# Weight conversion as single VectorE operations dealt over the mixing steps, VectorE in emission order, three softmax buffers

## The chip, the core and the metric

The kernel runs on one core of one Trainium2 chip. The metric is the device time of one launch in microseconds; lower is better. The core has a matmul engine (TensorE, PE in the rows, its weight loads PEld), VectorE (DVE), ScalarE (ACT), GpSimd (POOL) and SyncE (SP), which here only starts transfers. Each engine takes its own instructions in their order and waits on semaphores for the others.

## What is computed

Two blocks follow each other: an attention that mixes its heads before and after the softmax, and a Fourier mixing with a two-layer network behind it. Batch 8, 12 heads, 448 positions, 64 per head; so 768 channels, and 3072 in the hidden layer.

```python
scores = scale * np.matmul(q, k.transpose(0, 1, 3, 2))
scores = np.einsum('bhij,hg->bgij', scores, w_pre)
scores = scores - np.max(scores, axis=-1, keepdims=True)
attn = np.exp(scores)
attn = attn / (np.sum(attn, axis=-1, keepdims=True) + 1e-09)
attn = np.einsum('bhij,hg->bgij', attn, w_post)
x = np.matmul(attn, v)              # then (B, H, S, D) to (B, S, H*D)
...
X = np.fft.fft(x, axis=1)
X = np.fft.fft(X, axis=2)
u = x + np.real(X)
un = (u - mean(u)) / np.sqrt(var(u) + 1e-06)
out = u + np.maximum(un @ w_ch1, 0.0) @ w_ch2
```

The two weights of the network arrive as 64-bit numbers. The kernel makes 32-bit ones of them on the chip, by operations on the two halves of their bits, and keeps the result in device memory.

## The kernel before

The function `mix_phase` holds the attention, the Fourier mixing and the conversion of the weights; `ffn_phase` holds the network and comes behind it.

**Steps.** The mixing is cut into 192 steps (`TOT`), 24 for each of 8 batches. Step T has a tile of gathered score rows `Kr` (fetched from `Sb` by four transfers that SyncE starts, `emit_gather`), multiplied with `w_pre` on TensorE into the PSUM tile `mx` (*premix*, line 294). VectorE takes the row maximum of `mx` into `nmx` (line 301). ScalarE writes the exponentials into the softmax tile `PP`, with their sums in `den` (line 310). GpSimd adds the small constant to `den` (line 318), VectorE takes the reciprocal `rcp` (line 320), GpSimd scales `PP` with it (line 323). TensorE multiplies `PP` with `w_post` into `po` (*postmix*, line 333), and VectorE writes `po` transposed in blocks into `Pv` (line 344). `mx` and `po` have one buffer each, `PP` two, the PSUM tiles `ms` for everything else four.

**Order of emission.** The loop at the end of `mix_phase` emits step by step. In step s stand, in this order: premix, maximum and exponential of step s + 2 (`LM`), the score matmuls that are due (`emit_qk`, one in every step, two copies from `ms` to `Sb` behind each) or the value product (`emit_av`, every sixth step, copies to `XT`), the postmix and transpose of step s, the scaling of s + 2, the gather of s + 4, and then what is due of the rest: transposes of q and k (`emit_xpose`), the back-transposed output `X` (`emit_x`), the first Fourier transform (`emit_z`, line 416), and the second one with the sum to `X` (`emit_s2`: matmuls at line 436, four additions on VectorE at lines 444 and 447). Each batch has four of these sums, in four steps in a row early in the next batch; the text calls them sum steps. A step with none of the rest and no value product is called bare.

**Who sets the order.** `manual_schedule` keeps TensorE's instructions in the order of emission. On all other engines a scheduler sets the order ahead of time, by its own estimate of when operands are there.

**Copies.** `_Evac` chooses ScalarE or VectorE for the copies out of PSUM by a running sum for each engine. The conversion adds 440 to VectorE's sum for each of its operations.

**Conversion.** `_pieces` cuts the weights into 96 pieces of 128 rows by 384 (48 of `w_ch1`, then 48 of `w_ch2`). `emit_convert` has GpSimd start the load of a piece into `raw64` (line 457), then emits seven VectorE operations (lines 468 to 481) on the tiles `tmp` and `top`, and SyncE's transfer of `top` to `w1f` or `w2f` (line 483). The pool `pcv` has two buffers of each tile. Piece x is due at step 1.9 x (`WSTEP`); its seven operations are emitted together at the end of that step. On VectorE the scheduler moves them to where it expects operands.

## Time and profile before

| | us |
|---|---|
| three runs | 2999.58, 3004.24, 3007.17 |
| median | 3004.24 |
| profiled execution, its own time | 3000.97 |
| its span, first to last instruction | 2999.2 |
| TensorE busy in it | 2610.3 |
| VectorE busy | 1228.7 |
| ScalarE busy | 734.3 |
| GpSimd busy | 649.5 |
| mean granted TensorE clock, of full speed | 0.952 |

The profile is one execution. The page names lines of the kernel; a group of rows below says which view it is. In the timeline a row is a start, a duration, an engine, a line, an operation with its output and inputs, and in brackets the idle time of the engine ahead of it with what ended it. Rows of neighbouring equal instructions are merged (x4 is four). In the windows each engine has its busy time in the stretch, then come the clock that TensorE was granted (1.00 is full speed), the busy share of the DMA engines, and GB/s.

### The profile page before, as it was taken

Reading aid. Unit: us, or ns where it says so; the run is one execution under the profiler, and the core shown is the slowest. Engines: PE = TensorE matmul, PEld = TensorE weight load, DVE = VectorE, ACT = ScalarE, POOL = GpSimd, SP = SyncE. Lnnn points to the kernel's source line nnn. Section 1 sums busy time; section 2 is a strip of 40 time slices with the busy share of each in tenths; the row PEclk is TensorE's granted clock in tenths of the full one; section 3 lists DMA queues with packets and bytes.
Section 4 is the critical chain, followed back from the end, with each engine's and each line's share of the span. In section 5 each row is a group of like instructions: output and inputs, shape, how many; then the busy total and the mean of one; then the engine's idle time right before and its main releaser. Section 6 shows DMA issues by size and latency. Waiting matters only on the chain.

```text
span 2999.2 us, 47325 instructions
## 1 busy us (share of the span) xinstructions
PE 2610.3 (87%) x18992; PEld 1655.9 (55%) x18992; DVE 1228.7 (41%) x2242; ACT 734.3 (24%) x1931; POOL 649.5 (22%) x1101
## 2 busy tenths in 40 slices
PE   4565665979797988878999999999999999999998
PEld 1232322435344444435866866866876876876875
DVE  4878888644444444457430320320320320320220
ACT  2242232454545555531100100100100100100100
POOL 4353344353535434332001001001001001001000
PEclk8687887999999999988999999999999999999999
DMA  7566566443434333348544444444444444444432
GB/s 191 171 174 188 169 189 176 128 130 110 128 100 128 113 108 107 102 158 315 204 164 167 157 153 164 167 153 163 161 160 161 155 162 156 155 164 153 156 107 107
DMA packets 185112, 463.02 MB, mean 154 GB/s; under 512 B 22990, under 2 KB 128974, under 8 KB 172350
## 3 DMA queue, kind: packets, MB, share of 16 engines
q1 hardware_dynamic: 161886, 367.18, 35.4%
q0 software_dynamic: 23008, 92.82, 11.3%
q8 instruction: 151, 2.47, 0.3%
q14 instruction: 67, 0.55, 0.1%
HBM read 317.56 MB, written 59.77 MB: 126 GB/s over the span
## 4 chain that ended last, share of the span: by engine, by line
PE 41%; issue 11%; DMA 7%; ACT 2%; DVE 1%; SPq 1%; POOL 1%; ACTq 0%; POOLq 0%; DVEq 0%
PE psP L715 9%; PE psP L755 8%; PE psR L755 6%; PE psR L715 5%; PE psQ L755 3%; DMA w1t<-w1f 3%; PE psQ L715 2%; DMA out_dram<-u 2%; PE mx L294 1%; PE ms L436 1%; DMA w2t<-w2f 1%; DMA u<-u_scr 1%; ACT PP L310 1%; PE ms L268 1%; PE ms L361 1%
## 5 line engine op out<-in xcount | busy, mean ns | idle before, releaser
L715 PE MATMUL psP<-ub,w1t 128*128 128x256 f32 x2016 | 468.7, 386 | 26.8 <-DVE mv L674 15.1
L715 PEld LDWEIGHTS psP<-ub,w1t 128*128 128x128 f32 x2016 | 385.3, 193 | 95.3 <-DMA w1t<-w1f 24.4
L755 PE MATMUL psP<-w2t,h 128*128 128x384 f32 x1344 | 436.9, 486 | 0.0
L294 PE MATMUL mx<-Kr,kw 60*64 60x448 f32 x1536 | 209.0, 611 | 211.4 <-ACT PP L310 206.6
L755 PEld LDWEIGHTS psP<-w2t,h 128*128 128x128 f32 x1344 | 254.4, 190 | 173.4
L310 ACT ACTIVATE PP<-mx,nmx 128x448 f32<-128x448 f32 x384 | 240.2, 630 | 225.2 <-DVE nmx L301 194.1
L333 PE MATMUL po<-PP,kw 60*32 60x448 f32 x3072 | 209.8, 605 | 95.4 <-DVE Pv L344 71.9
L323 POOL TENSOR_SCALAR PP<-PP,rcp 128x448 f32<-128x448 f32 x384 | 252.8, 667 | 128.5 <-DVE rcp L320 123.8
L692 POOL TENSOR_TENSOR ub<-ub 128x768 f32<-128x768 f32 x28 | 50.8, 1837 | 1058.7 <-ACT ub L687 1058.2
L344 DVE STREAM_TRANSPOSE Pv<-po 128x896 f32<-128x896 f32 x192 | 213.6, 1112 | 157.1 <-PE po L333 157.1
L118 ACT COPY Sb<-ms 124x448 f32<-124x448 f32 x375 | 182.8, 541 | 308.3 <-PE ms L268 282.8
L301 DVE TENSOR_REDUCE nmx<-mx 128x2 f32<-128x896 f32 x192 | 208.6, 1086 | 113.1 <-PE mx L294 113.1
L715 PE MATMUL psR<-ub,w1t 128*128 128x256 f32 x1008 | 232.6, 380 | 0.4 <-DMA w1t<-w1s 0.3
L294 PEld LDWEIGHTS mx<-Kr,kw 60*64 60x64 f32 x1536 | 43.1, 140 | 321.9 <-ACT PP L310 298.8
L755 PE MATMUL psR<-w2t,h 128*128 128x384 f32 x672 | 220.0, 486 | 0.0
L268 PE MATMUL ms<-kT,qT 64*64 64x448 f32 (+1 forms) x1536 | 203.3, 589 | 4.6 <-DVE X L447 3.3
L715 PEld LDWEIGHTS psR<-ub,w1t 128*128 128x128 f32 x1008 | 190.9, 190 | 28.3 <-DMA w1t<-w1s 2.5
L755 PEld LDWEIGHTS psR<-w2t,h 128*128 128x128 f32 x672 | 126.3, 190 | 84.3
L764 DVE TENSOR_TENSOR u<-u,psP 128x384 f32<-128x384 f32 x56 | 31.0, 554 | 341.6 <-PE psP L755 341.6
L333 PEld LDWEIGHTS po<-PP,kw 60*32 60x32 f32 x3072 | 36.8, 109 | 237.0 <-issue 169.3
L361 PEld LDWEIGHTS ms<-Pv,vv 64*64 64x64 f32 x5376 | 154.4, 139 | 21.6 <-issue 17.7
L361 PE MATMUL ms<-Pv,vv 64*64 64x120 f32 x5376 | 157.5, 273 | 3.6 <-DVE Pv L344 1.9
(88 smaller groups left out, 2648.8 us busy)
## 6 DMA issues: line engine op xcount, KB each, us to landing
Kr<-Sb SPq DMA_DIRECT2D x768, 105.0 KB
w2t<-w2s SPq DMA_DIRECT2D x56, 1152.0 KB
w2t<-w2f SPq DMA_DIRECT2D x42, 1152.0 KB
w1t<-w1s SPq DMA_DIRECT2D x72, 576.0 KB
raw<-in_moe_w_ch_dram POOLq DMA_DIRECT2D x96, 384.0 KB, 4.0
w1t<-w1f SPq DMA_DIRECT2D x84, 384.0 KB
w1t<-w1f SPq DMA_DIRECT2D x96, 192.0 KB
w1t<-w1s SPq DMA_DIRECT2D x72, 192.0 KB
```

The lines of the kernel that those rows point to most:

```text
L118: self.nc.scalar.copy(out=out, in_=in_)
L268: nc.tensor.matmul(pss[x][64 * y:64 * y + r0 + 64 - lo, :S], st["qT", xx][64 * x:64 * x + 64, y, lo:r0 + 64], st["kT", xx][64 * x:64 * x + ...
L294: nc.tensor.matmul(mx[64 * z:64 * z + 64, x, :S], kw1[64 * x:64 * x + KR, :], Kr[64 * x:64 * x + KR, z, :], start=True, stop=True)
L301: nc.vector.tensor_reduce(nmx[:, :], steps[T]["mx"][:, :, :S], axis=AX.X, op=ALU.max, negate=True)
L310: nc.scalar.activation(PP[:, x, :], steps[T]["mx"][:, x, :S], ACTF.Exp, bias=steps[T]["nmx"][:, x:x + 1], accum_out=den[:, x:x + 1])
L323: nc.gpsimd.tensor_scalar(PP[:, x, :], PP[:, x, :], rcp[:, x:x + 1], 1.0, op0=ALU.mult, op1=ALU.mult)
L333: nc.tensor.matmul(po[o:o + 32, z, :S], kw2[64 * z:64 * z + KR, y, :], PP[64 * z:64 * z + KR, :, c * HS:(c + 1) * HS], start=True, stop=True)
L344: nc.vector.transpose(g["Pv"][:, T % GT, :].rearrange("p (z s) -> p z s", z=2), steps[T]["po"][:, :, :S])
L361: nc.tensor.matmul(pss[y][64 * x:64 * x + 64, pr * nu * R:(pr + 1) * nu * R], st["v"][64 * y:64 * y + 64, i, jb * D:(jb + 1) * D], _ap(Pv, ...
L692: nc.gpsimd.tensor_tensor(ub[:, o], ub[:, a], ub[:, b], op=ALU.subtract)
L715: nc.tensor.matmul(p, w[m][:, i, kc, :], ub[:, i, kc, :], start=opens and kc == 0, stop=kc == NK - 1, skip_group_check=True)
L755: nc.tensor.matmul(p, lhs[i][:, half * NQ + kf, x * P:(x + 1) * P], w[:, kf, :], start=opens and half == 0 and kf == 0, stop=half == 1 and ...
```

## The change

Three things are changed in `mix_phase`, and the function around it stays.

1. `emit_convert` gives back its seven operations one by one, and `convert(n)` emits the next n of the row of all pieces: the load of a piece is emitted ahead of its first operation, its store behind its last. From step -4 on, each step emits four, one of them between postmix and transpose, three behind the transpose and ahead of the scaling; in a sum step it emits one.
2. `manual_schedule` now names VectorE too, so its instructions stand as they are emitted. The copies and additions behind the rest (`take("full", ...)`) are put off in `pend`: they are emitted ahead of the next piece of the rest, or in the next step behind maximum and exponential.
3. The pool `ppp` of the softmax tile `PP` has three buffers in place of two.

```diff
@@ -52,7 +52,6 @@
 
 
 WC = 384
-WSTEP = 1.9
 
 TB = 512
 NTB = B * S // TB
@@ -147,7 +146,7 @@
     psb = pool("psb", 2)
     pkr = pool("pkr", 3)
     pvv = pool("pvv")
-    ppp = pool("ppp", 2)
+    ppp = pool("ppp", 3)
     psm = pool("psm", 4)
     ppv = pool("ppv", 2)
     pxt = pool("pxt")
@@ -161,6 +160,7 @@
     pms = pool("pms", 4, space=bass.MemoryType.PSUM)
 
     ev = _Evac(nc)
+    pend = []
 
     def ms_tile():
         return pms.tile([P, 512], F32, name="ms", tag="ms")
@@ -381,7 +381,8 @@
                     nc.scalar.copy(out=dst, in_=src)
                 else:
                     nc.vector.tensor_copy(out=dst, in_=src)
-        return [lambda y=y: done(y) for y in range(2)]
+        pend.extend(lambda y=y: done(y) for y in range(2))
+        return []
 
     def emit_x(g):
         X = pxx.tile([GR, DM], F32, name="X", tag="X")
@@ -462,27 +463,45 @@
         tmp = pcv.tile([P, WC], F32, name="tmp", tag="tmp")
         topb, tmpb = top[:, :].bitcast(U32), tmp[:, :].bitcast(U32)
 
-        def done():
-
-
-            nc.vector.tensor_scalar(tmpb, hi, 0x7fffffff, None, op0=ALU.bitwise_and)
-            nc.vector.tensor_scalar(tmp[:, :], tmp[:, :], _f32(0x38000000),
-                                    _f32(0x47efffff), op0=ALU.max, op1=ALU.min)
-
-            nc.vector.tensor_scalar(topb, tmpb, 0x07ffffff, 3, op0=ALU.bitwise_and,
-                                    op1=ALU.logical_shift_left)
-            nc.vector.scalar_tensor_tensor(topb, hi, 0xc0000000, topb,
-                                           op0=ALU.bitwise_and, op1=ALU.bitwise_or)
-
-            nc.vector.tensor_scalar(tmpb, topb, 0xff800000, None,
-                                    op0=ALU.bitwise_and)
-            nc.vector.scalar_tensor_tensor(tmp[:, :], lo, 2.0 ** -52, tmp[:, :],
-                                           op0=ALU.mult, op1=ALU.mult)
-            nc.vector.tensor_tensor(top[:, :], top[:, :], tmp[:, :], op=ALU.add)
+
+
+
+
+        vec = nc.vector
+        ops = [
+            lambda: vec.tensor_scalar(tmpb, hi, 0x7fffffff, None, op0=ALU.bitwise_and),
+            lambda: vec.tensor_scalar(tmp[:, :], tmp[:, :], _f32(0x38000000),
+                                      _f32(0x47efffff), op0=ALU.max, op1=ALU.min),
+            lambda: vec.tensor_scalar(topb, tmpb, 0x07ffffff, 3, op0=ALU.bitwise_and,
+                                      op1=ALU.logical_shift_left),
+            lambda: vec.scalar_tensor_tensor(topb, hi, 0xc0000000, topb,
+                                             op0=ALU.bitwise_and, op1=ALU.bitwise_or),
+            lambda: vec.tensor_scalar(tmpb, topb, 0xff800000, None,
+                                      op0=ALU.bitwise_and),
+            lambda: vec.scalar_tensor_tensor(tmp[:, :], lo, 2.0 ** -52, tmp[:, :],
+                                             op0=ALU.mult, op1=ALU.mult),
+            lambda: vec.tensor_tensor(top[:, :], top[:, :], tmp[:, :], op=ALU.add),
+        ]
+
+        def store():
             ev.d += 7 * 440.0
             nc.sync.dma_start(
                 out=dst, in_=top.rearrange("p (m f) -> p m f", m=split))
-        return [done]
+        return ops, store
+
+    cuts, conv = list(weights), []
+
+    def convert(n):
+
+        for _ in range(n):
+            if not conv and cuts:
+                ops, store = emit_convert(*cuts.pop(0))
+                conv.extend(ops)
+                conv.append(store)
+            if conv:
+                conv.pop(0)()
+            if len(conv) == 1:
+                conv.pop(0)()
 
 
     fill = {"tile": [], "full": [], "none": []}
@@ -512,42 +531,54 @@
             due("full", f + GS + 4 + x // 2,
                 lambda b=b, par=par, ch=ch: emit_z(b, par, ch))
     due("none", 2, emit_tables)
-    for x, cut in enumerate(weights):
-        due("none", x * WSTEP, lambda cut=cut: emit_convert(*cut))
     for v_ in fill.values():
         v_.sort(key=lambda e: (e[0], e[1]))
 
+    def flush():
+        while pend:
+            pend.pop(0)()
+
     def take(kind, s):
-        evs = []
+        n = 0
         while fill[kind] and fill[kind][0][0] <= s:
+            if kind == "full":
+                flush()
             evs = fill[kind].pop(0)[2]()
-            if kind == "none":
-                held.extend(evs)
+            n += 1
+            if kind == "full":
+                pend.extend(evs)
                 continue
             for fn in evs:
                 fn()
-
+        return n
+
+    sums = {f * GS + GS + 8 + n for f in range(B) for n in range(NG)}
     s = int(min(v_[0][0] for v_ in fill.values()))
-    with tc.manual_schedule(engines={mybir.EngineType.PE}):
+    with tc.manual_schedule(engines={mybir.EngineType.PE, mybir.EngineType.DVE}):
         while s < TOT or any(fill.values()):
-            held = []
             take("none", s)
             if 0 <= s + LM < TOT:
                 emit_premix(s + LM)
                 emit_max(s + LM)
                 emit_exp(s + LM)
+            flush()
             take("tile", s)
+            ops = 0 if s < -4 else 1 if s in sums else 4
             if 0 <= s < TOT:
                 emit_postmix(s)
+                convert(min(ops, 1))
                 emit_turn(s)
+                ops -= 1
+            convert(ops)
             if 0 <= s + LM < TOT:
                 emit_scale(s + LM)
             if 0 <= s + LG < TOT:
                 emit_gather(s + LG)
             take("full", s)
-            for fn in held:
-                fn()
             s += 1
+        flush()
+        while conv or cuts:
+            convert(1)
```

What the order of instructions is now, at three places. On VectorE around step 16 of the kernel before, two pieces of weights are converted side by side, as the scheduler set them (`nmx` is the maximum, `rcp` the reciprocal, `Pv` the transpose, all others are conversion):

```order
L344 STREAM_TRANSPOSE Pv_1105<-po_1247 128x896
L469 TENSOR_SCALAR tmp_3655<-tmp_3655 128x384
L320 RECIPROCAL rcp_1258<-den_1145 128x2
L472 TENSOR_SCALAR top_3654<-tmp_3655 128x384
L474 SCALAR_TENSOR_TENSOR top_3654<-raw64_3652,top_3654 128x384
L468 TENSOR_SCALAR tmp_3837<-raw64_3834 128x384
L477 TENSOR_SCALAR tmp_3655<-top_3654 128x384
L469 TENSOR_SCALAR tmp_3837<-tmp_3837 128x384
L301 TENSOR_REDUCE nmx_1276<-mx_1271 128x2
L479 SCALAR_TENSOR_TENSOR tmp_3655<-raw64_3652,tmp_3655 128x384
L472 TENSOR_SCALAR top_3836<-tmp_3837 128x384
L481 TENSOR_TENSOR top_3654<-top_3654,tmp_3655 128x384
```

In the later batches of the kernel before, nothing of this stands between the transposes, reciprocals and maxima. After the change, two steps of the sixth batch on VectorE:

```order
L320 RECIPROCAL rcp_8863<-den_8832 128x2
L301 TENSOR_REDUCE nmx_8877<-mx_8872 128x2
L477 SCALAR_TENSOR_TENSOR top_8857<-raw64_8855,top_8857 128x384
L344 STREAM_TRANSPOSE Pv_8562<-po_8892 128x896
L479 TENSOR_SCALAR tmp_8858<-top_8857 128x384
L481 SCALAR_TENSOR_TENSOR tmp_8858<-raw64_8855,tmp_8858 128x384
L483 TENSOR_TENSOR top_8857<-top_8857,tmp_8858 128x384
L320 RECIPROCAL rcp_8908<-den_8880 128x2
L301 TENSOR_REDUCE nmx_8922<-mx_8917 128x2
L472 TENSOR_SCALAR tmp_8948<-raw64_8945 128x384
L344 STREAM_TRANSPOSE Pv_8950<-po_8936 128x896
```

One piece at a time, four operations a step, the first between maximum and transpose, in every batch.

On ScalarE, around a value product in the middle of the mixing (`PP` is the exponential, `XT` the copies behind the value product, `Sb` the score copies). Before:

```order
L310 ACTIVATE PP_8916,den_8917<-mx_8909,nmx_8914 128x448 x2
L381 COPY XT_9054<-ms_8968 128x3x60
L381 COPY XT_9054<-ms_8969 128x3x60
L118 COPY Sb_8876<-ms_9059 124x448
L118 COPY Sb_8876<-ms_9060 124x448
L310 ACTIVATE PP_8964,den_8965<-mx_8957,nmx_8962 128x448 x2
```

After, the same place:

```order
L310 ACTIVATE PP_8924,den_8925<-mx_8917,nmx_8922 128x448 x2
L310 ACTIVATE PP_8972,den_8973<-mx_8965,nmx_8970 128x448 x2
L381 COPY XT_9062<-ms_8976 128x3x60
L381 COPY XT_9062<-ms_8977 128x3x60
L117 COPY Sb_8883<-ms_9063 124x448
L117 COPY Sb_8883<-ms_9064 124x448
```

The second exponential has moved ahead of the copies of the value product and of the scores.

On VectorE in a sum step late in the mixing (`X` are the four additions). Before:

```order
L320 RECIPROCAL rcp_13140<-den_13118 128x2
L444 TENSOR_TENSOR X_11817<-X_11817,ms_13154 112x385
L447 TENSOR_TENSOR X_11817<-X_11817,ms_13154 112x383
L444 TENSOR_TENSOR X_11817<-X_11817,ms_13149 112x385
L447 TENSOR_TENSOR X_11817<-X_11817,ms_13149 112x383
L301 TENSOR_REDUCE nmx_13176<-mx_13171 128x2
L344 STREAM_TRANSPOSE Pv_12858<-po_13190 128x896
```

After:

```order
L320 RECIPROCAL rcp_13134<-den_13104 128x2
L301 TENSOR_REDUCE nmx_13157<-mx_13152 128x2
L445 TENSOR_TENSOR X_11811<-X_11811,ms_13148 112x385
L445 TENSOR_TENSOR X_11811<-X_11811,ms_13143 112x385
L448 TENSOR_TENSOR X_11811<-X_11811,ms_13148 112x383
L448 TENSOR_TENSOR X_11811<-X_11811,ms_13143 112x383
L483 TENSOR_TENSOR top_13003<-top_13003,tmp_13004 128x384
L344 STREAM_TRANSPOSE Pv_12854<-po_13176 128x896
```

The maximum has moved ahead of the four additions, and one conversion operation stands behind them. That is so behind two of the four sum steps of a batch; behind the two others the additions stay ahead of the maximum.

## Rows read from the trace of the kernel before

**Rows 1.** The page, its first line.

```profile
span 2999.2 us, 47325 instructions
```

**Rows 2.** Timeline of VectorE: the transposes 0, 72, 168 and 191 of 192.

```profile
54.45 1.10 DVE L344 STREAM_TRANSPOSE Pv<-po 128x896 f32<-128x896 f32 x1
...
660.64 1.12 DVE L344 STREAM_TRANSPOSE Pv<-po 128x896 f32<-128x896 f32 x1 [0.54 <-PE po L333]
...
1216.32 1.12 DVE L344 STREAM_TRANSPOSE Pv<-po 128x896 f32<-128x896 f32 x1 [0.54 <-PE po L333]
...
1351.40 1.10 DVE L344 STREAM_TRANSPOSE Pv<-po 128x896 f32<-128x896 f32 x1
```

**Rows 3.** Windows: stretch, length; busy of PE, PEld, DVE, ACT, POOL; clock, DMA, GB/s.

```profile
200.00:300.00 100.00, 56.99 (x715) 24.04 (x723) 77.67 (x157) 30.17 (x83) 43.64 (x72) 0.76 0.63 178
900.00:1000.00 100.00, 84.79 (x1194) 44.07 (x1187) 44.21 (x61) 53.02 (x145) 44.20 (x83) 1.00 0.37 113
```

**Rows 4.** Line 468, first operation of a piece: ns min/median/max, first and last start.

```profile
L468 DVE TENSOR_SCALAR tmp<-raw x96: 317/360/1148, 31.2 to 549.6; 128x384 uint32<-128x384 uint32 x96
```

**Rows 5.** Waits, 0 to 550 us: who for whom, us in total, times, longest.

```profile
ACT PP L310 <- DVE nmx L301: 178.5, 42, 15.5
...
DVE tmp L468 <- DMA raw<-in_moe_w_ch_dram: 66.7, 56, 7.3
```

**Rows 6.** Timeline of a bare step in the last batch, rows of its chain and the scaling.

```profile
1310.42 0.98 PE L294 MATMUL mx<-Kr,kw 60*64 60x448 f32 x8 [0.75 <-ACT PP L310]
...
1311.04 1.25 POOL L323 TENSOR_SCALAR PP<-PP,rcp 128x448 f32<-128x448 f32 x2 [0.37 <-DVE rcp L320]
...
1311.55 1.09 DVE L301 TENSOR_REDUCE nmx<-mx 128x2 f32<-128x896 f32 x1 [0.68 <-PE mx L294]
...
1312.09 0.98 PE L333 MATMUL po<-PP,kw 60*32 60x448 f32 x16
1312.21 0.97 ACT L118 COPY Sb<-ms 124x448 f32<-124x448 f32 x2 [1.09 <-PE ms L268]
...
1313.23 0.64 ACT L310 ACTIVATE PP<-mx,nmx 128x448 f32<-128x448 f32 x1
...
1314.62 0.98 PE L294 MATMUL mx<-Kr,kw 60*64 60x448 f32 x8 [1.55 <-ACT PP L310]
```

**Rows 7.** Timeline of a step with a value product: maximum and its exponential.

```profile
1080.46 1.09 DVE L301 TENSOR_REDUCE nmx<-mx 128x2 f32<-128x896 f32 x1 [0.68 <-PE mx L294]
...
1086.56 0.64 ACT L310 ACTIVATE PP<-mx,nmx 128x448 f32<-128x448 f32 x1
```

**Rows 8.** Timeline of VectorE and GpSimd, a stretch with conversion.

```profile
283.37 0.36 DVE L472 TENSOR_SCALAR top<-tmp 128x384 uint32<-128x384 uint32 x1
283.65 0.16 DVE L320 RECIPROCAL rcp<-den 128x2 f32<-128x2 f32 x1
283.77 0.56 DVE L474 SCALAR_TENSOR_TENSOR top<-raw,top 128x384 uint32<-128x384 uint32 x1
284.00 1.56 POOL L323 TENSOR_SCALAR PP<-PP,rcp 128x448 f32<-128x448 f32 x2 [4.02 <-DVE rcp L320]
284.36 0.69 DVE L477 TENSOR_SCALAR tmp<-top 128x384 uint32<-128x384 uint32 x1
...
285.09 0.87 DVE L479 SCALAR_TENSOR_TENSOR tmp<-raw,tmp 128x384 f32<-128x384 uint32 x1
```

**Rows 9.** DMA issues: the load of a piece, KB, median us from issue to landing.

```profile
raw<-in_moe_w_ch_dram POOLq DMA_DIRECT2D x96, 384.0 KB, 4.0
```

**Rows 10.** Timeline of VectorE around a sum step.

```profile
1276.86 0.56 DVE L444 TENSOR_TENSOR X<-X,ms 112x385 f32<-112x385 f32 x1 [2.75 <-DMA Kr<-Sb]
...
1284.16 0.56 DVE L444 TENSOR_TENSOR X<-X,ms 112x385 f32<-112x385 f32 x1 [2.39 <-PE ms L436]
...
1286.03 1.08 DVE L301 TENSOR_REDUCE nmx<-mx 128x2 f32<-128x896 f32 x1
```

**Rows 11.** Windows of line 416 alone, one late batch: PE, PEld; clock, DMA, GB/s.

```profile
1077.81:1216.32 138.51, 11.66 (x56) 9.41 (x56) 1.00 0.33 106
```

## The prediction

> **What bounds the kernel now.** I read the page's first line, then transposes in the timeline, the windows, the waits, and at last single steps in the timeline. The span [rows 1] has two parts: a mixing part of 192 steps and a feed-forward part. The 192 transposes at line 344 mark the steps, one each: the first starts at 54.45, the last at 1351.40 [rows 2]. What comes behind, 2999.2 - 1351.4 = 1647.8 us, holds none of the moved work. Inside the mixing part the pace is not even. The first three batches of 24 steps take 660.64 - 54.45 = 606.2 us, 8.4 us a step; the four batches from there to 1216.32 take 555.7 us, 138.9 us each, 5.8 us a step [rows 2]. The windows say why [rows 3]: in the early one VectorE is busy 78 of 100 us and TensorE 57 at a granted clock of 0.76; in the late one VectorE 44 and TensorE 85 at 1.00, so at its upper level of 2.4 GHz. The conversion is the difference: its 96 first operations start between 31.2 and 549.6 [rows 4]. The waits there [rows 5] name the path: ScalarE's exponentials wait 178.5 us for `nmx`, the row maximum, whose reduction stands in VectorE's queue among conversion operations. So the early part is bound by VectorE's order, and the late part by TensorE and by the chain of one step.
>
> That chain is read from a bare step, one with no work but its own (11 of 24 in a late batch, two more nearly so). Premix starts at 1310.42, the next at 1314.62: 4.20 us [rows 6]. In between, the maximum runs 1311.55 to 1312.64, yet the exponential starts only at 1313.23: ScalarE has two score copies in front of it (to 1313.18), and the postmix that frees the softmax buffer ends at 1313.07. In a step with the value product the same wait is worse: the maximum was done at 1081.55, the exponential starts at 1086.56 [rows 7].
>
> **The change part by part.**
>
> *Conversion dealt out.* It removes no operation: 96 pieces of 7 operations are 672 before and after. Four now stand in each step, one in each of the four sum steps of a batch. Their price by rows: a two-source operation followed by one that depends on it takes 0.59 us from start to start (283.77 to 284.36), a single-source one its 0.36 and as much gap, 0.39 [rows 8]; seven make 3 x 0.59 + 4 x 0.39 = 3.3, four of them 1.9. Where the next operation doesn't depend, it starts 0.08 before the end (283.37 to 283.65), twice a step, so 1.7. A bare step then costs VectorE 1.00 (maximum) + 1.03 (transpose: 1.11 less 0.08) + 0.12 (reciprocal) + 1.7 = 3.85 us. In before's 4.20 the same engine had 2.2 of work; the idle rest hides the conversion.
>
> *GpSimd beside it.* The scaling at line 323 runs 1.25 us alone [rows 6] and 1.56 beside two conversion operations, which took 0.69 and 0.87 instead of 0.36 and 0.56 [rows 8]. In the new order the scaling starts after the reciprocal, then VectorE takes the maximum from PSUM, so only the first conversion operation meets its tail: 0 to 0.33 us a step, and I take 0.3: 4.15. A rule speaks against more of this: the Trainium skill, SBUF — State Buffer, in its section of terms, states that VectorE and GpSimd hold a shared pair of ports exclusively for a whole instruction and that the loser blocks fully. By that rule the operation would stand until the scaling is over, an estimated 0.45 us instead of 0.3, and the forecast would be some 14 us longer (95 bare steps by 0.15). The rows show the two operations stretched by 0.3 each, less than the 0.6 that one of the two scalings lasts.
>
> *Raw loads.* Each piece's load is issued by GpSimd, and VectorE now meets the first operation in fixed order. In the new order 86 of 96 loads stand at least one reciprocal ahead of their use; a load lands 4.0 us after issue [rows 9]. So the wait is 0 where a step lies between; upper bound the rate of before, 66.7 us [rows 5] over 96 pieces, 0.7 a piece, 0.4 a step. I take 0.25, nearer to zero because the lead is a full step. A bare step: 4.4, bounds 3.85 and 4.9.
>
> *Third softmax buffer.* The exponential needs no postmix of its own step any more, and the scheduler puts it ahead of the score copies in many steps and always ahead of the value product's copies. Chain without that wait: premix to maximum 1.13, maximum 1.09, exponential to next premix 1.39 (1313.23 to 1314.62) = 3.6 us [rows 6], below VectorE's 4.4; so in bare steps it buys nothing, VectorE is late next. In the value-product steps TensorE is next: premix would follow postmix at once, and the 1.39 from exponential to premix and the 0.16 from postmix to exponential leave the path. Two of four gain that 1.6 us, one in which key transposes fill TensorE about half, and the fourth, full of transform matmuls, nothing: 3.9 us a batch.
>
> *VectorE in emission order.* A sum step lasts 7.30 us (1276.86 to 1284.16), all matmuls, and its four additions to X take 1.87 (1284.16 to 1286.03), ahead of the maximum [rows 10]. In two of four sum steps the maximum now stands ahead of them. They then end 1.13 + 1.00 + 1.87 = 4.0 us after premix starts, and free the PSUM buffers for the next sum, which TensorE could begin at 1.67 + 0.91 = 2.6 (postmix starts 1.67 after premix and holds TensorE for some 0.9 of its 0.98) [rows 6, 10]. That costs 1.4 us twice a batch, 2.8. The score copies queued behind stay on ScalarE, as before.
>
> *SyncE.* 96 stores move between gathers, one for every 1.75 steps instead of two a step at the start; a gather has two steps of lead. I cost this at nothing; without that cover each late gather would hold the premix.
>
> The sum: a late batch becomes 138.9 - 3.9 + 2.8 + 13 x 0.2 = 140.4. The first batch has no batch before it: 138.9 less four sum steps (7.30 - 4.20 = 3.1 each, 12.4), less its transforms (11.7 of matmuls [rows 11], of which TensorE's spare 1.6 in each of four bare steps would hide 6.4: 5.3), less one value product (about 5 [rows 7]) = 116.2; then less 2.3 for its other products and 20 x 0.2 more for bare steps: 118. The last batch, 1351.40 - 1216.32 = 135.1 now, has conversion in two thirds of it: 137.5. Last transpose: 54.5 + 118 + 6 x 140.4 + 137.5 = 1152, where it was 1351.4. The gain is 199 us; 3001.0 of the profiled execution, 1.8 above its span, becomes **2802**. That execution lies 3.3 us under the median 3004.2, less than the range can notice.
>
> **The rivals.**
>
> *Better.* VectorE needs 3.85 in a bare step, loads never late, the sum's buffers free in time. First batch 107, middle 130.4 each, last 130.3: last transpose 1074, 277 us earlier, **2724**. For it: bare steps had VectorE idle half the time. Against: it wants every engine's queue in time.
>
> *Half clock.* If TensorE falls to its lower level, 1.2 GHz, in bare stretches, as in the early window's 0.76 [rows 3], its 2.6 us a step become 5.2 and bound it: 0.8 more in 20 steps of the first batch and 13 of each other. 1152 + 16 + 7 x 10.4 = 1241, **2891**. Against: late bare steps held 1.00 with the same 2.6 in 4.2.
>
> *The early pace has another cause* (start of the loads, low clock), and dealing the conversion out changes nothing there: the first three batches stay near 606, the others gain or lose 1.5 each: about **3005**. Against: the conversion's end and the drop to 4.20 lie together.
>
> *Slower.* A fixed order stops VectorE at a raw load that isn't there: transpose, reciprocal and maximum stand behind it, and TensorE waits for all of them. With the whole landing exposed, 4.0 us for each of 96 pieces, a third of it hidden in steps with long matmuls: 256 us against the gain of 199, **3058**. It decides from 199 / 96 = 2.1 us a piece on the path. For it: GpSimd issues between scalings that wait for VectorE. Against: the lead of a step, and waits of 0.7 a piece even where loads came two a step.
>
> **How the numbers follow.** Forecast 0.56, better 0.13, half clock 0.17, another cause 0.04, slower 0.05; 0.05 lies between the forecast and before, from several small waits. The range of the forecast by its own bounds, bare steps from 4.15 to 4.7, is 2775 to 2835; for 8 in 10 it must reach most of the better case and the half clock: 2730 to 2890. About 0.3% is what a measurement can tell from no change: faster 0.92, same 0.03, slower 0.05.
>
> **What would show it.** Transposes 24 to 168 should come 138 to 143 us apart by batch from the start, and the last near 1152; VectorE about 75% busy in all of the mixing part with granted clock 0.95 or more; the wait for `nmx` below 60 us; DMA waits at the first operation of a piece below 0.7 us each; the two sum steps 1.4 longer. It is wrong if bare steps take over 5 us, if the clock of the first 500 us stays below 0.9, or if the part behind the last transpose changes.

## The result, and the profile after

The changed kernel takes 2830.1 us (median of four runs, 2814.2 to 2837.5) where the kernel before takes 3001.9 beside it: a ratio of 0.942 (0.938 to 0.946). The forecast was 2802, 28 us too low; the gain is 172 us where 199 was forecast. The profiled execution took 2837.5, at the upper end of its runs.

The page of the changed kernel, its first lines (busy us, share, instructions of each engine):

```profile
span 2835.6 us, 47087 instructions
...
PE 2582.2 (91%) x18992; PEld 1652.4 (58%) x18992; DVE 1241.6 (44%) x2238; ACT 725.1 (26%) x1935; POOL 665.4 (23%) x1101
```

VectorE has as much work as before; it is spread differently. The timeline of the transposes after the change (numbers 0, 24, 72, 168 and 191), to be held against [rows 2]:

```profile
51.64 1.12 DVE L344 STREAM_TRANSPOSE Pv<-po 128x896 f32<-128x896 f32 x1
...
172.32 1.10 DVE L344 STREAM_TRANSPOSE Pv<-po 128x896 f32<-128x896 f32 x1
...
461.60 1.10 DVE L344 STREAM_TRANSPOSE Pv<-po 128x896 f32<-128x896 f32 x1
...
1045.81 1.10 DVE L344 STREAM_TRANSPOSE Pv<-po 128x896 f32<-128x896 f32 x1
...
1183.54 1.10 DVE L344 STREAM_TRANSPOSE Pv<-po 128x896 f32<-128x896 f32 x1
```

The first three batches take 410.0 us where they took 606.2. The slow early part is gone. But the six middle batches, 1 to 6, take 145.6 each (1045.81 - 172.32, by 6), where the forecast had 140.4 and the late batches before 138.9. Six times 5.2 is 31 of the 35 us by which the profiled execution lies over the forecast. The first batch (120.7 against 118), the last (137.7 against 137.5) and what follows the last transpose (2835.6 - 1183.5 = 1652.1 against 1647.8) hold 7 together, and the first transpose gives 3 back.

Windows after the change, the two stretches of [rows 3] and the six middle batches:

```profile
200.00:300.00 100.00, 89.69 (x1150) 47.67 (x1134) 63.39 (x109) 48.78 (x129) 49.50 (x87) 0.98 0.51 148
900.00:1000.00 100.00, 90.39 (x1145) 47.50 (x1144) 64.57 (x113) 45.26 (x126) 39.25 (x72) 0.98 0.49 146
...
172.32:1045.81 873.49, 746.37 (x9708) 374.89 (x9708) 613.88 (x1034) 432.44 (x1166) 431.49 (x754) 0.97 0.54 158
```

Early and late windows are alike now. VectorE is busy 70% in the middle batches (613.88 of 873.49), TensorE 85%, and the granted clock is 0.97.

Waits after the change from 60 to 1040 us (who for whom, us, times, longest), three rows against [rows 5]:

```profile
ACT PP L310 <- DVE nmx L301: 287.6, 154, 6.3
...
DVE tmp L472 <- DMA raw<-in_moe_w_ch_dram: 12.8, 11, 2.4
...
ACT Sb L117 <- DMA Kr<-Sb: 11.2, 2, 5.6
```

Raw loads are late 11 times, not 56 (11 of some 80 pieces in this stretch). The wait for the maximum has grown although the kernel is faster: the exponential now stands ahead of the score copies, so ScalarE waits for `nmx` with nothing else to do. Before, it was 172.5 us between 60 and 1210. The order is what moves it: in the changed kernel with two buffers (below), where the exponential stands behind the copies again, it is 2.5 us over the middle batches. A row of waits tells where an engine stands idle, not what the time hangs on.

### The profile page after: what moved, and what is told of

The parts are those of the page before. It is cut to its first block, busy times and chain, and to the rows that moved or that the text cites. A ratio compares the mean times of both kernels' runs of the same rounds, so it can differ in the third digit from the quotient of the medians.

```text
span 2835.6 us, 47087 instructions
## 1 busy us (share of the span) xinstructions
PE 2582.2 (91%) x18992; PEld 1652.4 (58%) x18992; DVE 1241.6 (44%) x2238; ACT 725.1 (26%) x1935; POOL 665.4 (23%) x1101
## 3 DMA queue, kind: packets, MB, share of 16 engines
q0 software_dynamic: 23008, 92.82, 12.1%
## 4 chain that ended last, share of the span: by engine, by line
PE 61%; issue 12%; DVE 11%; DMA 9%; ACT 3%; POOL 2%; SPq 1%; ACTq 0%; POOLq 0%; DVEq 0%
PE psP L746 10%; PE psP L786 10%; PE psR L786 7%; PE psR L746 6%; PE ms L437 5%; PE ms L361 4%; PE mx L294 4%; PE psQ L786 3%; DVE nmx L301 3%; PE ms L268 3%; PE po L333 3%; DMA w1t<-w1f 3%; PE ms L417 3%; PE psQ L746 2%; DVE Pv L344 2%
## 5 line engine op out<-in xcount | busy, mean ns | idle before, releaser
L333 PE MATMUL po<-PP,kw 60*32 60x448 f32 x3072 | 199.5, 573 | 7.5 <-DVE rcp L320 4.4
L718 ACT COPY ub<-psQ 128x384 f32<-128x384 f32 x56 | 24.9, 481 | 497.0 <-PE psQ L716 497.0
```

What stands on the lines that cost most here:

```text
L333: nc.tensor.matmul(po[o:o + 32, z, :S], kw2[64 * z:64 * z + KR, y, :], PP[64 * z:64 * z + KR, :, c * HS:(c + 1) * HS], start=True, stop=True)
```

## The experiments

Times are medians; each ratio is against the kernel before, run beside it. The changed kernel's own four runs lie up to 23 us apart, so a difference of a few us between two variants says nothing by itself. Lengths of batches come from the transposes of each profile, one execution of each kernel; that of the changed kernel is the slowest of its four. "Middle" is the mean of batches 1 to 6; for the first four kernels of the table, whose conversion ends early or lies early, it is that of batches 4 to 6, which hold none of it. A step is counted from one transpose to the next: sums are the four sum steps, products the four steps with a value product, behind are three of the steps right behind these (transposes 1 to 2, 13 to 14, 19 to 20), rest the other 13.

| kernel | us | ratio, 95% | first three batches | middle | sums | products | behind | rest |
|---|---|---|---|---|---|---|---|---|
| before | 3001.9 | 1 | 606.2 | 138.6 | 30.8 | 36.4 | 12.6 | 58.8 |
| buffer alone | 2965.5 | 0.985 to 0.988 | 593.1 | 132.4 | 29.5 | 32.2 | 10.5 | 60.2 |
| left to the scheduler | 2964.6 | 0.985 to 0.989 | 585.2 | 132.7 | 29.5 | 32.4 | 10.5 | 60.3 |
| fixed order, early | 2951.3 | 0.981 to 0.983 | 555.1 | 136.1 | 33.9 | 35.1 | 7.7 | 59.3 |
| **after** | 2830.1 | 0.938 to 0.946 | 410.0 | 145.6 | 33.9 | 36.4 | 12.1 | 63.2 |
| two buffers | 2849.2 | 0.947 to 0.950 | 416.2 | 146.7 | 31.5 | 37.6 | 12.6 | 65.0 |
| one operation | 2788.2 | 0.927 to 0.930 | 382.3 | 138.9 | 33.9 | 36.2 | 7.8 | 61.1 |
| fold apart | 2828.2 | 0.940 to 0.944 | 408.8 | 143.3 | 33.9 | 37.0 | 12.8 | 59.5 |
| fold on VectorE | 2830.4 | 0.941 to 0.945 | 410.4 | 145.1 | 33.9 | 36.4 | 12.1 | 62.7 |
| none between | 2848.8 | 0.947 to 0.950 | 420.2 | 147.4 | 33.9 | 38.4 | 11.3 | 63.7 |
| load ahead | 2834.9 | 0.941 to 0.945 | 410.6 | 146.3 | 33.9 | 37.0 | 12.1 | 63.3 |
| additions first | 2822.0 | 0.936 to 0.942 | 404.1 | 142.3 | 31.5 | 36.5 | 12.1 | 62.3 |
| in idle time | 2799.0 | 0.931 to 0.934 | 402.6 | 140.3 | 33.9 | 35.6 | 8.3 | 62.4 |
| idle, additions first | 2784.7 | 0.924 to 0.930 | 391.6 | 138.6 | 31.5 | 36.7 | 8.6 | 61.9 |

### Which of the three changes brings the gain

**The buffer alone**, in the kernel before:

```diff
-    ppp = pool("ppp", 2)
+    ppp = pool("ppp", 3)
```

> The kernel before with the third softmax buffer alone. If the gain comes from dealing the conversion out, the first three batches stay near 606 us, because VectorE's queue bounds them, and only the later value-product steps gain: at most 1.6 us in two of four of them in five batches, 16 us, so about 2985. If the buffer is what makes the difference (the exponential freed from the postmix), most of the 172 us comes with it alone: about 2830 to 2850.

2965.5. The early part stays slow, so the buffer isn't what makes the difference, but it is worth 41 us (3006.9 beside it to 2965.5), not 16: a late batch falls from 138.6 to 132.4.

**Two buffers**, in the changed kernel:

```diff
-    ppp = pool("ppp", 3)
+    ppp = pool("ppp", 2)
```

> The changed kernel with two softmax buffers again. The exponential of each step waits for a postmix again, so bare steps go from 4.0 back to 4.2 (some 95 steps, 19 us) and value-product steps from a median of 8.0 to 8.7 (21 steps, 14 us): about 2860 if the parts add up. If the buffer carries the gain, this is near 3000; if it is idle beside the dealing, 2830.

2849.2, 19 us more than with three. The same buffer is worth 41 us without the dealing and 19 with it; most of the gain comes with two buffers as well.

**The order left to the scheduler**, with the conversion emitted evenly and three buffers:

```diff
-    with tc.manual_schedule(engines={mybir.EngineType.PE, mybir.EngineType.DVE}):
+    with tc.manual_schedule(engines={mybir.EngineType.PE}):
```

> The changed kernel, but VectorE's order is left to the scheduler as before (only TensorE's is kept). The program emits the conversion evenly, yet the scheduler's order has the last piece of the 96 behind the 59th transpose again, where the changed kernel has it behind the 184th. If what counts is where the conversion stands on VectorE, the first three batches are near 600 us again and the time is about 2980 to 3000. If the single operations and the buffer are what counts, it is near 2830.

2964.6, what the buffer gives alone. Emitting four operations a step does nothing by itself: the scheduler draws them forward, and the first three batches take 585 us.

**The fixed order, but early:**

```diff
-            ops = 0 if s < -4 else 1 if s in sums else 4
+            ops = 0 if s < -4 else 1 if s in sums else 11
```

> The changed kernel with VectorE in order of emission, but eleven conversion operations in each step in place of four, so that the last piece stands behind the 64th transpose, as early as before the change. By the theory of the dealing VectorE has 11 x 0.47 = 5.2 us of conversion and 2.2 of its own in each such step, 7.4 and more against the 5.9 of a mean step now: 64 steps by 1.5 to 2.5 us, less some 25 us that the later batches get back without conversion: 2830 + 96 to 160 - 25 = about 2900 to 2965. If the fixed order by itself is the gain, 2830 or less.

2951.3, inside what the theory of the dealing gave. A fixed order with the conversion bunched is slow too. So the gain needs both halves of the edit: the even dealing, and an order that keeps it. Together they are 135 us (2965.5 to 2830.1), the buffer 41.

In these slow kernels the transfers of the conversion are early too, so they are a rival to VectorE's order. No run moves the loads without the operations; the chain that ended last tells them apart in part. For the fixed order, early, it lies from 60 to 550 us about half on VectorE, 11.5% on raw loads and not at all on the gathers; for the buffer alone, a third on VectorE and 30% on raw loads. So with the buffer alone a good part of the early time is a load that VectorE's queue stands behind. In the changed kernel the same stretch is 54% on TensorE, a quarter on VectorE, and raw loads have no part that shows.

### What makes the middle batches longer

This kernel also gives the price of the dealing. Its batches 4 to 6 have the fixed order, three buffers and no conversion: 136.1. With the conversion the batch is 145.6, so it costs 9.5 us a batch (8.8 over the same batches 4 to 6). Some 2.5 of that lie in four single steps of the six batches: two with a hole in TensorE's stream and two in which a score copy waits for a gather (both further down) are 3 to 4.7 us longer than the median of their kind.

**One operation** in place of seven:

```diff
-        ops = [
...
+        ops = [lambda: None] * 6 + [
+            lambda: vec.tensor_scalar(topb, hi, 0x7fffffff, None, op0=ALU.bitwise_and),
         ]
```

> The changed kernel with six of the seven conversion operations of each piece left out (loads and stores stay, in the same places, so the weights are wrong). It asks what the dealt-out conversion still costs. In the kernel with the fixed order and the early conversion, batches 4 to 6, which have no conversion left, take 136.1 us on average; the changed kernel's middle batches 145.6. If VectorE's operations are the price, the middle batches come down to 136 to 138 and the time to 2830 - 7 x 8.5 = about 2770. If loads and stores (transfers that meet the gathers) or holes in TensorE's stream are the price, it stays within 15 us of 2830.

2788.2, and 138.9 a middle batch, a little over the 136 to 138 expected. Six operations are 6.7 of the 9.5; loads, stores and the last operation are the other 2.8. In the table most of the 6.7 lies in one column: the three steps behind a value product take 7.8 us without the operations and 12.1 with them. If each of the 24 steps is taken by its median over the batches, so that single long steps drop out, it is plainer: 135.4 without conversion, 137.0 with one operation, 141.9 with seven, and of these last 4.9 the three steps have 4.3.

The rows show why. Timeline of VectorE (and the postmix of the second step) behind a value product, fixed order without conversion:

```profile
901.50 1.12 DVE L344 STREAM_TRANSPOSE Pv<-po 128x896 f32<-128x896 f32 x1 [5.13 <-PE po L333]
...
902.59 1.06 DVE L301 TENSOR_REDUCE nmx<-mx 128x2 f32<-128x896 f32 x1
...
902.99 0.98 PE L333 MATMUL po<-PP,kw 60*32 60x448 f32 x16
...
904.08 1.12 DVE L344 STREAM_TRANSPOSE Pv<-po 128x896 f32<-128x896 f32 x1 [0.43 <-PE po L333]
```

And the same place in the changed kernel:

```profile
618.68 1.12 DVE L344 STREAM_TRANSPOSE Pv<-po 128x896 f32<-128x896 f32 x1 [3.65 <-PE po L333]
...
619.73 0.52 DVE L481 SCALAR_TENSOR_TENSOR tmp<-raw,tmp 128x384 f32<-128x384 uint32 x1
...
620.17 0.98 PE L333 MATMUL po<-PP,kw 60*32 60x448 f32 x16
620.27 0.56 DVE L483 TENSOR_TENSOR top<-top,tmp 128x384 f32<-128x384 f32 x1
...
620.75 0.35 DVE L472 TENSOR_SCALAR tmp<-raw 128x384 uint32<-128x384 uint32 x1
...
621.11 1.06 DVE L301 TENSOR_REDUCE nmx<-mx 128x2 f32<-128x896 f32 x1
...
622.09 0.66 DVE L473 TENSOR_SCALAR tmp<-tmp 128x384 f32<-128x384 f32 x1
...
622.67 1.10 DVE L344 STREAM_TRANSPOSE Pv<-po 128x896 f32<-128x896 f32 x1
```

With three buffers the exponentials are ready ahead, and TensorE does premix and postmix of the next step at once. Without conversion the next transpose comes 2.58 us later. With it VectorE works without a gap for 3.99 us: the postmix ended at 621.15, and `po` waits 1.5 us for VectorE. And 3.65 us of VectorE ahead of the first transpose, while TensorE was at the value product, are idle. The conversion stands on the wrong side of that transpose.

**The fold apart.** GpSimd folds `X` in four steps of a batch, beside conversion operations; this variant takes those behind the transpose away there:

```diff
+            if s > 2 and s % GS in (2, 14, 20):
+                ops = 1
+            elif s % GS in (0, 1, 5, 6, 12, 13, 17, 18, 23):
+                ops = 5
```

> The changed kernel, with no conversion operation behind the transpose in the three steps of a batch ahead of which GpSimd folds X (steps 2, 14, 20), and five in place of four in nine other steps. If an operation of VectorE's stands still while GpSimd folds (one took 1.56 us there instead of 0.36), steps 3 and 15 come back from 5.4 and 4.8 to 4.2 each, less 9 x 0.3 us where a fifth operation lengthens a bare step, at least half of which lies beside TensorE's work: 1 to 1.5 us a batch less, so 2820 to 2825. If those steps are long for another reason, 2835 to 2850, by the fifth operations.

2828.2, no difference by the time. But the edit does more than it was meant to: the nine steps with five operations are met in the steps ahead of step -4 as well, where the changed kernel emits none. So 38 operations stand ahead of the first maximum in place of 8, and the first transpose comes 10.4 us later than in the changed kernel:

```profile
62.05 1.12 DVE L344 STREAM_TRANSPOSE Pv<-po 128x896 f32<-128x896 f32 x1 [0.79 <-PE po L333]
```

The middle batches are 2.3 shorter by their mean, and as long as those of the changed kernel by the medians of the steps (142.0 and 141.9). So the time hides a late start, and what is gained behind it lies in single long steps. Step 3 did not come back: the operation I had left between maximum and transpose met the fold. Timeline of that place in this variant, GpSimd and VectorE:

```profile
631.44 1.25 POOL L323 TENSOR_SCALAR PP<-PP,rcp 128x448 f32<-128x448 f32 x2
...
632.37 2.78 DVE L477 SCALAR_TENSOR_TENSOR top<-raw,top 128x384 uint32<-128x384 uint32 x1
...
632.64 0.18 POOL L403 COPY xe<-X 112x2 f32<-112x2 f32 x1
632.79 0.99 POOL L406 TENSOR_TENSOR xo<-X 112x383 f32<-112x383 f32 x1
...
633.74 0.99 POOL L404 TENSOR_TENSOR xe<-X 112x383 f32<-112x383 f32 x1
...
635.07 1.10 DVE L344 STREAM_TRANSPOSE Pv<-po 128x896 f32<-128x896 f32 x1
```

An operation of 0.56 us takes 2.78: it is over 0.4 us after GpSimd's last one, and the transpose stands behind it.

**The fold on VectorE** takes the collision away (the diff puts `nc.vector` for `nc.gpsimd` in the three operations of the fold):

```diff
-            nc.gpsimd.tensor_tensor(xe[:, 1:DH], X[:, 1:DH], X[:, DM - 1:DH:-1],
+            nc.vector.tensor_tensor(xe[:, 1:DH], X[:, 1:DH], X[:, DM - 1:DH:-1],
```

> The changed kernel with the fold of X (three operations in four steps of a batch) on VectorE in place of GpSimd. It costs VectorE 32 x 1.1 = 35 us of work, and nothing of GpSimd's then lies beside a conversion operation but the scalings; the raw loads, which GpSimd starts, no longer stand behind the fold. If the fold held VectorE's operations up, step 3 goes from 5.36 to at most 4.7, step 15 from 4.84 to at most 4.6, and no operation beside them takes over 0.9 us: 0 to 1.5 us a batch less, 2818 to 2830. If the fold did no harm, those steps grow by up to 1.1 each: 2840 to 2860.

2830.4. Over all 672 conversion operations, what they take beyond their usual durations falls from 66 to 34 us (summed from the timeline's rows), and the time doesn't move: step 3 stays at 5.3, step 15 goes from 4.7 to 5.5. Less stretching and the fold's 49 us of work on VectorE come out even; this run can't tell the two apart.

**None between** maximum and transpose, where the scaling's tail stretches an operation:

```diff
                 emit_postmix(s)
-                convert(min(ops, 1))
                 emit_turn(s)
-                ops -= 1
             convert(ops)
```

> The changed kernel with all four conversion operations of a step behind the transpose, none between maximum and transpose. The forecast held that the operation between them meets the scaling on GpSimd and is stretched by 0.3 us in every bare step; in the profile of the changed kernel 116 of 672 conversion operations are stretched beside the scaling. If that is a price on the path, bare steps go from 4.1 to 3.8 and the time to 2830 - 13 x 0.3 x 7.5 = about 2800. If the stretch is covered there (the transpose would wait for the postmix or the maximum for the premix anyway), no change: 2820 to 2840. In value-product steps one operation less lies in VectorE's idle time, 21 x 0.5 = 10 us against it.

2848.8, 19 us slower, with only 14 us of stretching left of 66. So taking the stretching away did not bring the 30 us that I had expected; this run moves the operations as well, so it doesn't say what the stretching alone costs. Where the 19 us come from the table says in part: 2.0 a batch in the product steps, where the operation between had lain in idle time. Several other steps take 5.97 us. In the timeline of one of these the premix comes after a wait for the exponential and runs at half its speed (1.77 for 0.98), and so do the matmuls behind it:

```profile
570.92 1.77 PE L294 MATMUL mx<-Kr,kw 60*64 60x448 f32 x8 [2.11 <-ACT PP L310]
...
572.47 1.72 PE L268 MATMUL ms<-kT,qT 64*64 64x448 f32 x8
...
574.11 1.04 PE L333 MATMUL po<-PP,kw 60*32 60x448 f32 x16
```

The granted clock over the middle batches of this variant is 0.95, against 0.97. What starts those waits, no run here settles.

**Load ahead.** The load of a piece is started when the piece before it begins:

```diff
...
+                if cuts:
+                    ahead.append(emit_convert(*cuts.pop(0)))
...
```

> The changed kernel with each piece's load started one piece ahead, and nothing else; the kernel with the conversion in VectorE's idle time had this as well, and this run tells the two edits apart. VectorE waits 12.8 us for raw loads in 11 places of the middle batches now, 1.2 us in one place of that other kernel. If the placing is what brought the 31 us there, this one gains at most those 12 us: 2818 to 2830. If the late loads, by the steps they upset, are the price, it comes near 2800.

2834.9. VectorE's wait for loads falls from 12.8 us to 3.3, and the time stays. Loads are not the price.

**Additions first** in the sum steps:

```diff
             take("full", s)
+            if s in sums:
+                flush()
```

> The changed kernel, with the four additions to X emitted directly behind each sum's matmuls, ahead of the next maximum, in all four sum steps. The forecast had 2.8 us a batch for their place behind the maximum, and the profile shows the four sum steps 3.1 us longer than before. If their place is the reason, the four steps go from 33.9 back to about 30.8 and the time to 2830 - 7 x 3.1 = 2808. If it is the conversion operations in them, no change; if the maximum is now late by 1.9 us and that counts more, 2840 or more.

The sum steps go from 33.9 to 31.5 a batch, 2.4 of the 3.1. By times the effect is at the edge of the noise: 2822.0, runs from 2810 to 2828, against 2814 to 2838. The rows show the mechanism. A sum step of the changed kernel, then of this variant:

```profile
679.77 1.09 DVE L301 TENSOR_REDUCE nmx<-mx 128x2 f32<-128x896 f32 x1 [3.78 <-PE mx L294]
...
680.78 1.14 DVE L445 TENSOR_TENSOR X<-X,ms 112x385 f32<-112x385 f32 x2
...
681.83 1.13 DVE L448 TENSOR_TENSOR X<-X,ms 112x383 f32<-112x383 f32 x2
...
682.43 2.85 PE L437 MATMUL ms<-tce,z 97*112 97x385 f32 x8 [1.14 <-DVE X L448]
```

```profile
670.41 1.15 DVE L445 TENSOR_TENSOR X<-X,ms 112x385 f32<-112x385 f32 x2 [2.17 <-PE ms L437]
...
671.48 1.13 DVE L448 TENSOR_TENSOR X<-X,ms 112x383 f32<-112x383 f32 x2
672.53 1.08 DVE L301 TENSOR_REDUCE nmx<-mx 128x2 f32<-128x896 f32 x1
672.88 2.85 PE L437 MATMUL ms<-tce,z 97*112 97x385 f32 x8
```

Behind the maximum the additions free the PSUM tiles late, and TensorE waits 1.14 us for them; ahead of it, it doesn't wait.

### The conversion in VectorE's idle time

Seven operations ahead of the transpose in value-product steps and two behind it, five or six behind it in sum and transform steps, none where the fold is, one elsewhere; loads one piece ahead:

```diff
...
-            ops = 0 if s < -4 else 1 if s in sums else 4
+            pre, ops = (0, 0 if s < -4 else 4) if s < 1 else (
+                (7, 2) if s % GS in (1, 7, 13, 19) else
+                (0, 5) if s % GS in (8, 9, 10, 11) else
+                (0, 6) if s % GS in (4, 5, 6) else
+                (0, 0) if s % GS in (2, 14, 20) else (0, 1))
...
                 emit_postmix(s)
-                convert(min(ops, 1))
+                convert(pre)
                 emit_turn(s)
-                ops -= 1
             convert(ops)
```

> The changed kernel, with the same 84 conversion operations a batch put where VectorE waits for TensorE: seven between maximum and transpose in the four value-product steps and two behind, five or six behind the transpose in sum and transform steps, none where GpSimd folds X, and one in every other step; each piece's load is started one piece ahead. If an operation costs time only where VectorE is the bound of its step (bare steps took 3.4 us on average without conversion, 4.2 with four operations), the middle batches come to 136 to 139 us and the time to about 2770 to 2790. If the price is one of the amount, of transfers or of holes in TensorE's stream, it stays at 2815 to 2845.

2799.0, 31 us less than the changed kernel, and 140.3 a middle batch. Load ahead alone gained nothing, so it is the placing. VectorE in a value-product step of this kernel:

```profile
598.27 0.56 DVE L483 TENSOR_TENSOR top<-top,tmp 128x384 f32<-128x384 f32 x1
...
598.76 0.35 DVE L472 TENSOR_SCALAR tmp<-raw 128x384 uint32<-128x384 uint32 x1
...
601.16 0.56 DVE L481 SCALAR_TENSOR_TENSOR tmp<-raw,tmp 128x384 f32<-128x384 uint32 x1
...
603.33 1.12 DVE L344 STREAM_TRANSPOSE Pv<-po 128x896 f32<-128x896 f32 x1 [1.61 <-PE po L333]
```

Seven operations run between 598.27 and 601.72, and VectorE still waits 1.61 us for the postmix. The three steps behind take 8.3 us in place of 12.1: 3.8 of the 5.3 us by which the batch is shorter. By the medians of the steps the batch is 139.7, so 2.2 shorter: some other steps, which now hold more operations, are longer, and the rest of the 5.3 are single long steps, which were fewer or shorter. The stretching beside GpSimd is lower here too, 19 us for 66; how much of the gain that is, no run separates.

**Both together**, this and the additions first:

> Both that helped in one: the conversion where VectorE waits for TensorE (2799 by itself), and the additions to X directly behind their sums (the four sum steps went from 33.9 to 31.5). In the first of these kernels the sum steps take 33.9 as well. If the two are independent, 2799 - 7 x 2.4 = 2782, faster than both kernels of this case. If the five conversion operations behind the transpose in each sum step now delay additions that stood behind the maximum, the gain is halved or gone: 2790 to 2800.

2784.7 (2774.7 to 2792.7), a ratio of 0.927 (0.924 to 0.930): the fastest complete kernel of this case, 45 us under the changed one. The two gains add up, within the 18 us by which its runs differ.

## Why the prediction was right, and where its sum was off

**The bound and its cure were right.** The early part was bound by VectorE's order. With the conversion early in VectorE's queue the first three batches stay at 555 to 606 us, with two buffers or three and whoever sets the order; dealt out, they take 410, or 416 with two buffers. So the rival of another cause fell. How much of that early time VectorE's queue only stands behind raw loads (above), these runs don't separate. Nor do they hold the clock fixed: between 200 and 300 us it was 0.76 before, 0.74 with the fixed order, early, and 0.98 dealt out, so part of the dealing's gain is TensorE at its upper level. The forecast's first batch, last batch and tail hold within 5 us each, the first of them by luck: with one operation of seven it takes 109.1, so the other six cost 11.6 there, where I had 4 for all of them.

**The failing step is the third buffer's, together with the price of a bare step.** I worked out a gain of 3.9 a batch for the value-product steps "because TensorE is next", and a price of 13 x 0.2 for conversion against before's 4.20. Both meet in the same place. Built up from the runs, a middle batch is 138.6 before; - 6.2 by the buffer (buffer alone); + 3.7 by the fixed order (fixed order, early); + 2.8 by transfers and one operation, + 6.7 by the other six (one operation): 145.6. The forecast had 138.9 - 3.9 + 2.8 + 2.6. So the buffer gave more than I thought, the order cost nearly what I thought, and conversion cost 9.5 where I had 2.6. My price was the rise over a step of 4.20, but the buffer lowers the step that conversion must hide in: to 2.58 behind a value product. There VectorE's 3.85 us of work, which I had worked out myself, is the bound (3.99 measured), and takes back 4.4 of the buffer's gain. Product steps and the three behind them go from 49.0 to 48.5, where I had a gain of 3.9.

That the time still came within 28 us is in part luck: the buffer's gain, 2.3 a batch larger than forecast, offset a third of the 6.9 by which conversion was too cheap. 2830 lies inside the range of 2730 to 2890, and at the upper end of 2775 to 2835, the forecast's own bounds. By the medians of the steps conversion costs 6.5 a batch; the forecast had no term for the single long steps that make up the rest.

**Bare steps of 4.4** were too dear where nothing disturbs them: 3.9 to 4.4 by their medians. But steps 3 and 4 average 5.4 and 5.6, 15 and 21 4.7 and 5.4.

**GpSimd beside it: 0.3 us a step.** The stretching is there, 153 of 672 operations by 66 us together, but no run shows it as a term of the sum: with 14 us of it left the time was 19 longer, with 34 left the same, and both runs changed something else with it. The rule that I weighed, of the Trainium skill, SBUF — State Buffer, section of terms (the loser of the shared ports blocks fully), agrees with the row of 2.78 us better than a mere slowing does; the 14 us that I worked out from it do not show.

**Raw loads: 0.25 a step.** 12.8 us between 60 and 1040, over some 80 pieces, so 0.16 a piece; taking most of it away gained nothing. The rival that loads would make it slower fell with that.

**Emission order: 2.8 a batch.** The sum steps are 3.1 longer, the two in which I had placed the wait by 1.3 and 1.0. The wait is 1.14 where I had 1.4, and the cure gives 2.4 back. Right.

**SyncE at nothing.** Nearly. Twice in the middle batches a score copy waits for a gather that still reads its `Sb` buffer, and an exponential stands behind it. ScalarE and TensorE of the changed kernel there:

```profile
735.47 0.53 ACT L117 COPY Sb<-ms 124x448 f32<-124x448 f32 x1 [5.64 <-DMA Kr<-Sb]
735.90 0.64 ACT L310 ACTIVATE PP<-mx,nmx 128x448 f32<-128x448 f32 x1
...
737.30 1.77 PE L294 MATMUL mx<-Kr,kw 60*64 60x448 f32 x8 [4.31 <-ACT PP L310]
```

The two steps take 7.4 and 7.6 instead of 4.3, 6 us in all. Whether the stores between the gathers cause it was not tried.

**Half clock** came in single steps, not in stretches: 0.97 over the middle batches where late batches had 1.00. The premix of 1.77 us behind the gather's wait above is one of them. It is part of the spread between batches (143.1 to 149.4), not a cause of its own that a run separated.

**Signs.** The batches came 143.1 to 149.4 us apart, not 138 to 143, and the last transpose at 1183.5, not near 1152. VectorE 70% busy for 75 forecast, the clock above 0.95, loads below 0.7 us a piece, two sum steps longer: as forecast but for the size. The wait for `nmx` below 60 us was wrong as a sign: 287.6, for the reason given with the rows.

## What to carry to other kernels

Work that only fills an engine should be placed by where that engine waits, not in equal shares: the same 84 operations a batch were 31 us cheaper where VectorE stood waiting for TensorE. An order emitted by hand holds only on engines whose order is really kept; left to the scheduler, the evenly emitted work went back to the front. When two edits are made at once, price the second against the step that the first one leaves: a buffer that shortens a step takes away the idle time in which the other edit was to hide.

## What the runs showed of the hardware

**One operation of VectorE can be held for several of GpSimd's.** In the rows around the one of 2.78 us four GpSimd operations follow each other with no gap, the second scaling (from 632.06) and the three of the fold; VectorE's, started during the first of them, is over only 0.42 us after the last. I had expected one such operation to be waited for at most.

**Holes in TensorE's stream.** A run of matmuls, nearly always a value product, now and then stops for 1 to 3 us in which the engine waits for no semaphore that the profile shows. The changed kernel:

```profile
286.87 3.09 PE L361 MATMUL ms<-Pv,vv 64*64 64x120 f32 x107
292.43 2.51 PE L361 MATMUL ms<-Pv,vv 64*64 64x120 f32 x59 [2.47 <-issue]
```

That step takes 12.3 us where others of its kind take 8.1. In the hole one packet of the queue for instructions is under way; the DMA view of 289.6 to 291.0 (packets, MB, share of the engines):

```profile
q8 instruction: 1, 0.02, 5.2%
```

In the kept trace this packet of 16 KB runs from 289.68 to 290.85, and TensorE goes on 1.57 us later. That is so each time: between first and last transpose, TensorE stops 47 times in the 14 kernels for over 0.3 us with no semaphore that the profile shows, and each of these stops ends 1.2 to 1.8 us after the end of such a packet, a stretch that by chance would hold one in twenty. So the holes are waits for the engine's own instructions, as far as a coincidence that never fails can show it; why some packets come late was not tried.

There are 19 holes of over 1 us in the middle batches of the ten kernels that have conversion there (some 8600 us), and none in the 1620 us of batches 4 to 6 of the four others. They don't need the conversion, though: the kernel before and the one with the buffer alone have one each in batch 3, 1.25 and 1.70 us, when their conversion is over. Before:

```profile
776.65 0.88 PE L361 MATMUL ms<-Pv,vv 64*64 64x120 f32 x25 [1.25 <-issue]
```

All 21 lie in the step of a batch's third or fourth value product. Whether conversion makes them more frequent or longer, these counts don't settle.
